# A fused retention and two-layer MLP kernel: part of the first layer by seven half-size products, with sums of x on GpSimd and two x tiles

## Chip, cores and metric

The kernel runs on one core of one Trainium2 chip. The metric is the device time of one execution in microseconds (us). A core has a matrix engine (TensorE, "PE" in the profile), VectorE ("DVE"), ScalarE ("ACT"), GpSimd ("POOL"), and SyncE ("SP"), which issues most of the transfers here.

## Reference

Eight batches of eight heads go through retention, a linear attention with a decay per head; the result, 4608 tokens of 512 features, goes through two matrix products with a leaky ReLU between them.

```python
def _attn_ref(q, k, v):            # q, k, v: (8, 8, 576, 64) float32
    scale = 1.0 / np.sqrt(D_)
    scores = scale * np.matmul(q, k.transpose(0, 1, 3, 2))
    gamma = 1.0 - 2.0 ** (-5.0 - np.arange(H))
    rel = pos[:, None] - pos[None, :]
    Dmat = np.where(rel >= 0, gamma[:, None, None] ** rel[None, :, :], 0.0)
    return np.matmul(scores * Dmat[None], v)

def _moe_ref(x, w_in, w_out):      # x: (4608, 512), w_in: (512, 2048), w_out: (2048, 512)
    h = x @ w_in
    g = np.maximum(0.01 * h, h)
    return g @ w_out
```

The inputs and the output are float32; the kernel multiplies in float16 and accumulates in float32.

## The kernel before

**Units and groups.** The tokens are cut into 36 units of 128 (two chunks of 64) and 9 groups of 512 (four units). Retention runs unit by unit and the MLP group by group. Everything is in one hand-written order; each engine executes its own instructions in that order, and semaphores join the engines where data passes. A pool hands out its buffers in turn, and a new tile waits until the old one in its buffer has been read.

**Retention of a unit u.** `load` (line 119) fetches k, q and v, from unit 8 on through SP. `cast_k` (172, ScalarE), `cast_q` (175) and `cast_v` (179) turn them into float16, the last two with decay factors; from unit 8 on these two run on GpSimd. `transpose_dma` (181) transposes q and k by a transfer on SP. `scores` (218, 227) makes the score blocks and the state updates on TensorE, `masks` (236) and `state` (258 to 264) take them up on VectorE, and `state_cast` (276, 279) makes the float16 state. `outputs` (294, 305) multiplies by v and by the state; `own` (361, ScalarE) and `add` (366, VectorE) put the two parts together into the tile xT of the group, one of three buffers of `x_pool` (73). `burst(u)` (682) is scores of u with outputs of u - 1 and the VectorE, GpSimd and ScalarE work that follows; `step(u)` (710) is the burst, the loads of unit u + 4, and `ahead(u + 2)` (697): k cast, q cast, v cast, transpose. Units 0 to 7 are transposed on TensorE in an order of their own, in which `settle` (661) is the VectorE work on a unit's states and masks.

**First layer.** `h_block(g, f)` (395) makes one of 16 blocks of 128 hidden features for 512 tokens: four matmuls of 512 columns into one of four PSUM buffers of `acc_pool` (80), then `leaky` on ScalarE (393) into the tile gt. Groups 0 and 1 use `h_half` (256 tokens, two blocks) and `h_unit` (128 tokens, four blocks) instead. All of them record line 379 for their matmuls.

**Second layer.** Group 0 uses `wide` (429, 16 calls of four matmuls). From group 1 on, `seven` (475) forms the product of a 2 by 2 block matrix with a 2 by 2 block matrix by seven half-size products instead of eight, in the manner of Strassen and Winograd. It needs sums of the hidden tile (`mix`, 473, VectorE), sums of the output weights (`mix_weights`, 454), and intermediate sums k1, u2, v kept in SBUF. Each product is 16 times two matmuls of 256 columns (493). Product p1 is copied to k1 by ScalarE (505) before a second product is accumulated on top of it. `hooks` place a step after the first product and another after the fifth.

**Main loop.** For groups 2 to 8 the order of the first layer is blocks in pairs (i, i + 8), a step of the next group's units after the 5th and the 13th block, the mixes of the first half after the 9th, then `seven`. In a group g the steps are those of units 4g + 5, 4g + 6, and, in `seven`, 4g + 7 and 4g + 8. Ahead of the loop, `early(12, 14)` in the hooks of group 1 does burst 12, the casts and the transpose of unit 14, and then the loads of unit 16.

**Start of the main part.** After the blocks of groups 0 and 1 (lines 718 to 790), 16 `wide` calls follow with work attached by number in the dictionary `at` (797): for example scores of unit 8 after call 4 and `early(9, 12)` after call 9. Loads of units 8 to 11 and the transposes of 8 and 9 are put among the last blocks of group 1:

```python
    halves(1, (1, 4))
    load(10)
    ahead(8)
```

Of the kernel before, what the change touches and what calls it, by code (L numbers as in the profile page):

```python
# [9 lines left out]
FP = mybir.dt.float32  # L10
# [8 lines left out]
def kernel(  # L19
# [9 lines left out]
    nc = tc.nc  # L29
# [40 lines left out]
    ld_pool = ctx.enter_context(tc.tile_pool(name="ld", bufs=6))  # L70
    a_pool = ctx.enter_context(tc.tile_pool(name="ap", bufs=4))
    b_pool = ctx.enter_context(tc.tile_pool(name="bp", bufs=2))
    x_pool = ctx.enter_context(tc.tile_pool(name="xp", bufs=3))
    g_pool = ctx.enter_context(tc.tile_pool(name="gp", bufs=2))
    s_pool = ctx.enter_context(tc.tile_pool(name="sp", bufs=1))
    o_pool = ctx.enter_context(tc.tile_pool(name="op", bufs=3))
# [27 lines left out]
    w_in16 = const_pool.tile([P, NP, DFF], F16, name="w_in16")  # L104
    w_out16 = const_pool.tile([P, NF, DM], F16, name="w_out16")
    w_mix = const_pool.tile([P, 4, HF, HN], F16, name="w_mix")
    zst = const_pool.tile([P, NP, CH], F16, name="zst")
    idle = const_pool.tile([P, TOK], F16, name="idle")

# [9 lines left out]
    def load(u, eng=None, after=None):  # L119
        for x in (1, 0, 2):  # L120
            t = ld_pool.tile([P, H, D], FP, name=f"t32_{x}")
            t32[u, x] = t
            c = 2 * u
            same = c % CB + 1 < CB
            e = eng[x] if isinstance(eng, dict) else eng or nc.sync
            engs = e if isinstance(e, tuple) else (e,)
            n = H // len(engs)
            for j, rows in ((0, P),) if same else ((0, CH), (1, CH)):
                b, w = (c + j) // CB, (c + j) % CB
                for i, e in enumerate(engs):  # L130
                    hs = slice(n * i, n * i + n)
                    d = e.dma_start(
                        out=t[CH * j : CH * j + rows, hs],
                        in_=(q, k, v)[x][b, hs, CH * w : CH * w + rows, :].rearrange(
                            "h t d -> t h d"
                        ),
                    )
                    if after is not None and (x in after or not isinstance(after, dict)):
                        behind(d, *(after[x] if isinstance(after, dict) else after))
                        after = None  # L140
                    last_load[u, x] = d
# [28 lines left out]
    def cast_k(u):  # L170
        qk16[u] = a_pool.tile([P, 2, H, D], F16, name="qk16")
        nc.scalar.copy(out=qk16[u][:, 1], in_=t32[u, 1])  # L172

    def cast_q(u, eng):
        eng.tensor_tensor(out=qk16[u][:, 0], in0=t32[u, 0], in1=decay(u, 0), op=MUL)  # L175

    def cast_v(u, eng):
        v16[u] = a_pool.tile([P, H, D], F16, name="v16")
        eng.tensor_tensor(out=v16[u], in0=t32[u, 2], in1=decay(u, 1), op=MUL)  # L179

    def transpose_dma(u):
        qkT[u] = a_pool.tile([P, 2, NP, P], F16, name="qkT")
        nc.sync.dma_start_transpose(
            out=qkT[u].rearrange("p x c t -> p (x c) t"),
            in_=qk16[u].rearrange("t x h d -> t (x h d)"),
        )
# [205 lines left out]
    def leaky(out, in_):  # L392
        nc.scalar.activation(out=out, in_=in_, func=mybir.ActivationFunctionType.Lrelu)  # L393
# [13 lines left out]
    def h_unit(u, fb):  # L407
        g, t0 = u // 4, (u % 4) * P
        ts = slice(t0, t0 + P)
        hps = acc_pool.tile([P, 4, P], FP, name="acc")  # L410
        for n in range(4):
            h_mm(hps, n, g, 4 * fb + n, ts)
        leaky(g_tile(g)[:, 4 * fb : 4 * fb + 4, ts], hps)

    def store(g, a, osb):
        r0 = g * TOK + a * HT
        nc.sync.dma_start(
            out=out[r0 : r0 + HT, :].rearrange("(t p) d -> p t d", p=P), in_=osb  # L420
        )
# [24 lines left out]
    def mix_weights(n, x):  # L446
        fs = slice(x * HF // 2, (x + 1) * HF // 2)
        a, b = (
            (w_part(0, 1), w_part(0, 0)),
            (w_part(1, 1), w_mix[:, 0]),  # L450
            (w_part(1, 1), w_part(0, 1)),
            (w_part(1, 0), w_mix[:, 1]),
        )[n]
        nc.vector.tensor_tensor(out=w_mix[:, n, fs], in0=a[:, fs], in1=b[:, fs], op=SUB)
# [6 lines left out]
    def mix(g, n, x):  # L461

        fs = slice(x * HF // 2, (x + 1) * HF // 2)
        if g not in sums:
            sums[g] = s_pool.tile([P, 2, HF, HT], F16, name="mix")
        s = sums[g]
        z, a, b, op = (
            (s[:, 0], g_part(g, 1, 0), g_part(g, 1, 1), ADD),
            (s[:, 1], s[:, 0], g_part(g, 0, 0), SUB),
            (g_part(g, 1, 0), g_part(g, 0, 0), g_part(g, 1, 0), SUB),  # L470
            (g_part(g, 0, 0), g_part(g, 0, 1), s[:, 1], SUB),
        )[n]
        nc.vector.tensor_tensor(out=z[:, fs], in0=a[:, fs], in1=b[:, fs], op=op)  # L473
# [175 lines left out]
    def halves(g, *items):  # L649
        for a, fb in items:  # L650
            h_half(g, a, fb)

    def cast_qv(u):
        cast_q(u, nc.vector)
        cast_v(u, nc.vector)
# [5 lines left out]
    def settle(u):  # L661
        state(u, 0)
        state_cast(u, dve_copy, (0,))
        masks(u)
        state(u, 1)
# [11 lines left out]
    def mixes(g, *ns):  # L677
        for n in ns:
            mix(g, n, 0)
            mix(g, n, 1)  # L680
# [13 lines left out]
            own(u - 1)  # L694
            add(u - 1)

    def ahead(u):

        if u >= NU:
            return  # L700
        cast_k(u)
        cast_q(u, nc.gpsimd)
        cast_v(u, nc.gpsimd)
        transpose_dma(u)

    def fetch(u):
        if u < NU:
# [2 lines left out]
    def step(u):  # L710
        burst(u)
        fetch(u + 4)
        ahead(u + 2)


    halves(0, (0, 1))
# [34 lines left out]
    turn(6, 0)  # L751
    h_unit(5, 0)
    scores(6)
    settle(6)
    cast_qv(7)
    h_unit(5, 1)
    turn(7, 1)
    halves(1, (0, 4))
# [15 lines left out]
    mix_weights(0, 0)  # L774
    mix_weights(0, 1)
    h_unit(7, 0)
    h_unit(7, 1)
    mix_weights(1, 0)
    mix_weights(1, 1)
    halves(1, (1, 4))  # L780
    load(10)
    ahead(8)
    mix_weights(2, 0)
    mix_weights(2, 1)
    halves(1, (1, 5), (1, 6))
    ahead(9)
    load(11)
    mix_weights(3, 0)
    mix_weights(3, 1)
    halves(1, (1, 7))  # L790

    def early(u, n):
        burst(u)
        ahead(n)
        load(n + 2)

    at = {
# [2 lines left out]
        3: lambda: mixes(1, 1),  # L800
        4: lambda: (burst(8, False), ahead(11), load(13)),
        7: lambda: mixes(1, 2),
        9: lambda: early(9, 12),
    }
    for n in range(16):
# [3 lines left out]
    burst(10)  # L809
    seven(1, {0: [lambda: early(11, 13)], 4: [lambda: early(12, 14)]})  # L810

    first = [f for i in range(4) for f in (i, i + HF)]
    second = [f for i in range(4, 8) for f in (i, i + HF)]
    for g in range(2, NG):
        more = g < NG - 1
        for n, f in enumerate(first + second):
            h_block(g, f)
            if more and n in (4, 12):
                step(4 * g + 5 + (n == 12))
            if n == 8:  # L820
                for m in range(3):
                    mix(g, m, 0)
        for m in range(3):
            mix(g, m, 1)
        seven(
            g,
            {0: [lambda: step(4 * g + 7)], 4: [lambda: step(4 * g + 8)]} if more else {},
            g == NG - 1,
        )
# [30 lines left out]
```

## Time and profile before

| | |
|---|---|
| median of 8 runs | 289.54 us (289.35 to 291.73) |
| the profiled execution, its own time | 289.65 us |
| span of its profile, first to last instruction | 287.9 us |
| mean granted TensorE clock | 0.998 of full speed |
| busy PE / DVE / ACT / POOL | 279.3 / 173.0 / 143.9 / 104.7 us |
| first-layer matmuls, 512 columns (L379) | 448, record 379 ns each |
| second-layer matmuls, 256 columns (L493) | 896, record 273 ns each |
| activation of a block (L393) | 144, 597 ns each |
| GpSimd q cast / v cast (L175, L179) | 1087 / 1140 ns mean |
| from one group's first layer to the next | 29.11 us |

A record of a matmul contains its way through the pipeline; matmuls in a row overlap, so their true cost is the distance from one start to the next. In the chain of waits, a piece is given by its start, its length, the engine with the tile written and the line, and the number of instructions. In the timeline, a row is start, length, engine, line, operation, out<-in, count, and in brackets the idle time before it with what ended it. A "q" after an engine's name is its queue or sequencer. "DMA" is the mean busy share of the 16 transfer engines in tenths of each of 40 slices.

### The profile page before, as it was taken

Reading aid. Unit: us, or ns where it says so; the run is one execution under the profiler, and the core shown is the slowest. Engines: PE = TensorE matmul, PEld = TensorE weight load, DVE = VectorE, ACT = ScalarE, POOL = GpSimd, SP = SyncE. Lnnn points to the kernel's source line nnn. Section 1 sums busy time; section 2 is a strip of 40 time slices with the busy share of each in tenths; the row PEclk is TensorE's granted clock in tenths of the full one; section 3 lists DMA queues with packets and bytes.
Section 4 is the critical chain, followed back from the end, with each engine's and each line's share of the span. In section 5 each row is a group of like instructions: output and inputs, shape, how many; then the busy total and the mean of one; then the engine's idle time right before and its main releaser. Section 6 shows DMA issues by size and latency. Waiting matters only on the chain.

```text
span 287.9 us, 9432 instructions
## 1 busy us (share of the span) xinstructions
PE 279.3 (97%) x4111; PEld 190.4 (66%) x4111; DVE 173.0 (60%) x297; ACT 143.9 (50%) x254; POOL 104.7 (36%) x124
## 2 busy tenths in 40 slices
PE   8899999999999999999999999999999999999994
PEld 3478889545874587458745874587458745874584
DVE  2884687984664585459545863586368636740352
ACT  4676766623237633763277327732773176317510
POOL 8979502745333333333434333234325413000000
PEclk9999999999999999999999999999999999999999
DMA  8999999999999999956897679766976251012003
GB/s 215 300 238 213 292 206 201 199 165 236 201 253 288 220 209 201 260 130 148 184 257 160 140 159 278 148 148 152 285 156 147 49 173 39 3 68 81 0 2 146
DMA packets 131738, 50.01 MB, mean 174 GB/s; under 512 B 121264, under 2 KB 126000, under 8 KB 131696
## 3 DMA queue, kind: packets, MB, share of 16 engines
q1 hardware_dynamic: 125392, 39.59, 59.8%
q0 software_dynamic: 6016, 9.70, 14.9%
q8 instruction: 32, 0.52, 0.7%
q10 hardware_dynamic: 288, 0.11, 0.2%
q14 instruction: 10, 0.08, 0.1%
HBM read 36.81 MB, written 9.44 MB: 161 GB/s over the span
## 4 chain that ended last, share of the span: by engine, by line
PE 86%; DMA 5%; DVE 5%; ACT 1%; issue 1%; POOL 1%; POOLq 0%; DVEq 0%
PE acc L379 41%; PE acc L493 34%; DMA t<-in_q_dram 4%; PE acc L429 3%; PE sc L218 3%; DMA qkT<-qk 2%; PE ot L294 2%; PE sc L227 1%; PE ot L305 1%; PE acc L200 1%; DVE qk L175 1%; DVE st L279 1%; DVE s L236 1%; DVE s L260 1%; DVE xT L366 0%
## 5 line engine op out<-in xcount | busy, mean ns | idle before, releaser
L379 PE MATMUL acc<-xT,w_in 128*128 128x512 f16 (+2 forms) x768 | 131.0, 326 | 0.2 <-DVE xT L366 0.2
L393 ACT ACTIVATE gt<-acc 128x512 f16<-128x512 f32 x144 | 85.9, 597 | 56.7 <-PE acc L379 55.1
L379 PEld LDWEIGHTS <-w_in 128*128 128x128 f16 x768 | 68.1, 98 | 51.5
L493 PEld LDWEIGHTS <-gt 128*128 128x128 f16 x640 | 61.8, 98 | 9.2
L236 DVE TENSOR_TENSOR s<-sc,cs 128x512 f16<-128x512 f32 x34 | 23.3, 686 | 39.2 <-PE sc L227 39.2
L493 PE MATMUL acc<-w_out,gt 128*128 128x256 f16 x384 | 45.9, 273 | 0.2
L276 POOL CAST st<-s 128x512 f16<-128x512 f32 x21 | 12.8, 609 | 89.8 <-DVE s L260 56.4
L361 ACT COPY own<-ot 128x512 f32<-128x512 f32 x33 | 19.3, 585 | 42.4 <-PE ot L305 35.0
L175 POOL TENSOR_TENSOR qk<-t,cs 128x512 f16<-128x512 f32 x28 | 30.4, 1087 | 18.8 <-ACT gt L393 15.4
L179 POOL TENSOR_TENSOR v<-t,cs 128x512 f16<-128x512 f32 x28 | 31.9, 1140 | 1.5 <-DMA t<-in_v_dram 1.5
L473 DVE TENSOR_TENSOR mix<-gt 128x1024 f16<-128x1024 f16 x16 | 14.0, 878 | 28.8 <-ACT gt L393 28.8
L493 PE MATMUL acc<-w_mix,gt 128*128 128x256 f16 x256 | 30.6, 273 | 0.0
L493 PE MATMUL acc<-w_mix,mix 128*128 128x256 f16 x256 | 29.5, 273 | 0.0
L493 PEld LDWEIGHTS <-mix 128*128 128x128 f16 x256 | 24.9, 98 | 3.1 <-DVE mix L473 0.2
L172 ACT CAST qk<-t 128x512 f16<-128x512 f32 x36 | 22.3, 620 | 7.9 <-DMA t<-in_k_dram 5.5
L366 DVE TENSOR_TENSOR xT<-ot,own 128x512 f16<-128x512 f32 x33 | 22.6, 683 | 5.1 <-ACT own L361 5.1
L260 DVE TENSOR_TENSOR s<-sc,s 128x256 f32<-128x256 f32 x37 | 15.5, 419 | 1.7 <-PE sc L227 1.1
L218 PEld LDWEIGHTS <-qkT 64*64 64x64 f16 x576 | 7.7, 107 | 12.6 <-issue 9.9
L519 DVE TENSOR_TENSOR osb<-acc,u 128x512 f32<-128x512 f32 (+1 forms) x17 | 11.2, 656 | 7.9 <-PE acc L493 7.9
L473 DVE TENSOR_TENSOR mix<-mix,gt 128x1024 f16<-128x1024 f16 x16 | 14.8, 932 | 0.5
L279 POOL CAST st<-s 128x256 f16<-128x256 f32 x7 | 3.2, 454 | 31.3 <-DVE s L264 19.4
L429 PE MATMUL acc<-w_out,gt 128*128 128x512 f16 x64 | 14.3, 380 | 0.0
(57 smaller groups left out, 236.5 us busy)
## 6 DMA issues: line engine op xcount, KB each, us to landing
out_dram<-osb SPq DMA_DIRECT2D x17, 512.0 KB, 3.9
t<-in_k_dram SPq DMA_DIRECT2D x27, 256.0 KB, 4.4
t<-in_q_dram SPq DMA_DIRECT2D x26, 256.0 KB, 4.1
t<-in_v_dram SPq DMA_DIRECT2D x25, 256.0 KB, 4.9
w_in<-in_moe_w_in_dram POOLq DMA_DIRECT2D x8, 256.0 KB, 6.4
w_out<-in_moe_w_out_dram POOLq DMA_DIRECT2D x4, 512.0 KB, 10.9
t<-in_v_dram POOLq DMA_DIRECT2D x7, 256.0 KB, 5.5
t<-in_q_dram POOLq DMA_DIRECT2D x6, 256.0 KB, 5.6
```

Source lines behind the costliest of these rows:

```text
L172: nc.scalar.copy(out=qk16[u][:, 1], in_=t32[u, 1])
L175: eng.tensor_tensor(out=qk16[u][:, 0], in0=t32[u, 0], in1=decay(u, 0), op=MUL)
L179: eng.tensor_tensor(out=v16[u], in0=t32[u, 2], in1=decay(u, 1), op=MUL)
L236: nc.vector.tensor_tensor(out=s16s[u], in0=sc_tiles[u][:, :, 0], in1=mask_sb.unsqueeze(1).unsqueeze(1).to_broadcast([P, 2, NP, CH]), op=MUL,)
L260: nc.vector.tensor_tensor(out=to, in0=st, in1=carry[0], op=ADD)
L361: nc.scalar.copy(out=owns[u], in_=ot_tiles[u][:, :, 0:NP].rearrange("q j c t -> q c j t"))
L366: nc.vector.tensor_tensor(out=x_of(u).rearrange("q (c g) t -> q c g t", g=2), in0=ot_tiles[u][:, :, NP : 2 * NP].rearrange("q g (c j) t -> ...
L379: nc.tensor.matmul(out=hps[:, n, :], lhsT=w_in16[:, c, f * P : (f + 1) * P], rhs=xT[g][:, c, ts], start=(c == 0), stop=(c == NP - 1),)
L393: nc.scalar.activation(out=out, in_=in_, func=mybir.ActivationFunctionType.Lrelu)
L429: nc.tensor.matmul(out=ys[tb], lhsT=g_t[0][:, f, tb * P : (tb + 1) * P], rhs=w_out16[:, f, :], start=(f == 0), stop=(f == NF - 1),)
L473: nc.vector.tensor_tensor(out=z[:, fs], in0=a[:, fs], in1=b[:, fs], op=op)
L493: nc.tensor.matmul(out=r[name][tb][:, 0, :] if apart else r[name][0][:, tb, :], lhsT=lhs[:, f, tb * P : (tb + 1) * P], rhs=rhs[:, f, :], s ...
```

## The change

In groups 2 to 8 four of the sixteen first-layer blocks, 0, 1, 8 and 9, are made by `h_seven`: the 2 by 2 block product of w_in (features 0-1 or 8-9; contraction chunks 0-1 or 2-3) with x (the two contraction halves; the two token halves of 256), by seven products of 2 x 2 matmuls with 256 columns. Four more blocks stand between the products. It reads four sums of weight blocks, which `sum_w_in` makes once on VectorE after wide call 12, and four sums of x, which `sum_x` makes on GpSimd for each group, in the step that completes its x: after that step's q cast and ahead of its v cast. Three intermediate sums, and h4 (twice) and h5, are formed by VectorE; ScalarE applies the activation from PSUM once and from SBUF three times. `x_pool` goes from three buffers to two. The steps of the main loop stand after the first eight blocks and after the 14th, the first half's mixes after the 11th. The casts and transposes of units 8 and 9 and the loads of 10 and 11 around them are put earlier among the blocks of group 1, the transpose of 8 ahead of the loads of 10. In place of `settle(6)` and the casts of q and v of unit 7, the q cast is put between the masks of unit 6 and its second state.

```diff
-    x_pool = ctx.enter_context(tc.tile_pool(name="xp", bufs=3))
+    x_pool = ctx.enter_context(tc.tile_pool(name="xp", bufs=2))
...
+    w_sum = const_pool.tile([P, 4, NP // 2, 2 * P], F16, name="w_sum")
...
+    def w_sub(i, j):
+        return w_in16[:, 2 * j : 2 * j + 2, i * HF * P : i * HF * P + 2 * P]
+
+    def x_sub(g, j, k):
+        return xT[g][:, 2 * j : 2 * j + 2, k * HT : (k + 1) * HT]
+
+    def sum_w_in(n):
+        a, b, op = (
+            (w_sub(1, 0), w_sub(1, 1), ADD),
+            (w_sum[:, 0], w_sub(0, 0), SUB),
+            (w_sub(0, 0), w_sub(1, 0), SUB),
+            (w_sub(0, 1), w_sum[:, 1], SUB),
+        )[n]
+        nc.vector.tensor_tensor(out=w_sum[:, n], in0=a, in1=b, op=op)
+
+    x_sums = {}
+
+    def sum_x(g):
+        x_sums[g] = t = s_pool.tile([P, 4, NP // 2, HT], F16, name="x_sum")
+        for n, (a, b) in enumerate(
+            (
+                (x_sub(g, 0, 1), x_sub(g, 0, 0)),
+                (x_sub(g, 1, 1), t[:, 0]),
+                (x_sub(g, 1, 1), x_sub(g, 0, 1)),
+                (x_sub(g, 1, 0), t[:, 1]),
+            )
+        ):
+            nc.gpsimd.tensor_tensor(out=t[:, n], in0=a, in1=b, op=SUB)
+
+    def h_seven(g, fill):
...
+        def product(name, lhs, rhs, fresh):
+            if fresh:
+                r[name] = acc_pool.tile([P, 2, HT], FP, name="acc")
+            for n in range(2):
+                for c in range(NP // 2):
+                    nc.tensor.matmul(
...
+        def plus(name, a, b):
+            r[name] = m_pool.tile([P, 2, HT], FP, name=name)
+            nc.vector.tensor_tensor(out=r[name], in0=r[a], in1=r[b], op=ADD)
+
+        def give(i, k, name):
+            leaky(g_tile(g)[:, i * HF : i * HF + 2, k * HT : (k + 1) * HT], r[name])
+
+        product("p1", w_sub(0, 0), x_sub(g, 0, 0), True)
+        r["k1"] = m_pool.tile([P, 2, HT], FP, name="k1")
+        nc.scalar.copy(out=r["k1"], in_=r["p1"])
+        h_block(g, fill[0])
+        product("p1", w_sub(0, 1), x_sub(g, 1, 0), False)
+        give(0, 0, "p1")
+        h_block(g, fill[1])
+        product("p6", w_sum[:, 1], t[:, 1], True)
+        plus("u2", "p6", "k1")
+        product("p5", w_sum[:, 0], t[:, 0], True)
+        plus("v", "p5", "u2")
+        h_block(g, fill[2])
+        product("p7", w_sum[:, 2], t[:, 2], True)
+        plus("h4", "p7", "v")
+        product("p5", w_sum[:, 3], x_sub(g, 1, 1), False)
+        plus("h5", "p5", "u2")
+        give(1, 1, "h4")
+        h_block(g, fill[3])
+        give(0, 1, "h5")
+        product("p7", w_sub(1, 1), t[:, 3], False)
+        plus("h4", "p7", "u2")
+        give(1, 0, "h4")
...
-    def ahead(u):
...
+    def ahead(u, between=None):
+
+        if u < NU:
+            cast_k(u)
+            cast_q(u, nc.gpsimd)
+        if between is not None:
+            between()
+        if u < NU:
+            cast_v(u, nc.gpsimd)
+            transpose_dma(u)
...
-        ahead(u + 2)
+        ahead(u + 2, (lambda: sum_x(u // 4 - 1)) if u % 4 == 0 else None)
...
-    settle(6)
-    cast_qv(7)
+    state(6, 0)
+    state_cast(6, dve_copy, (0,))
+    masks(6)
+    cast_q(7, nc.vector)
+    state(6, 1)
+    cast_v(7, nc.vector)
...
     h_unit(7, 0)
+    ahead(8)
+    load(10)
     h_unit(7, 1)
     mix_weights(1, 0)
     mix_weights(1, 1)
-    halves(1, (1, 4))
-    load(10)
-    ahead(8)
+    halves(1, (1, 4), (1, 5))
     mix_weights(2, 0)
     mix_weights(2, 1)
-    halves(1, (1, 5), (1, 6))
     ahead(9)
     load(11)
+    halves(1, (1, 6))
...
-        ahead(n)
+        ahead(n, (lambda: sum_x(u // 4 - 1)) if u % 4 == 0 else None)
...
+        12: lambda: [sum_w_in(n) for n in range(4)],
...
-    first = [f for i in range(4) for f in (i, i + HF)]
-    second = [f for i in range(4, 8) for f in (i, i + HF)]
+    rest = [f for i in range(2, HF) for f in (i, i + HF)]
     for g in range(2, NG):
         more = g < NG - 1
-        for n, f in enumerate(first + second):
+        h_seven(g, rest[:4])
+        if more:
+            step(4 * g + 5)
+        for n, f in enumerate(rest[4:]):
             h_block(g, f)
-            if more and n in (4, 12):
-                step(4 * g + 5 + (n == 12))
-            if n == 8:
+            if n == 2:
                 for m in range(3):
                     mix(g, m, 0)
+            if more and n == 5:
+                step(4 * g + 6)
```

More of the change, by code (lines that the diff above doesn't have):

```diff
@@ new lines @@
+    x_sums = {}
[11 more added lines that the diff above has]
+    def h_seven(g, fill):
+        r = {}
+        t = x_sums[g]
+        def product(name, lhs, rhs, fresh):
[4 more added lines that the diff above has]
+                    nc.tensor.matmul(
+                        out=r[name][:, n, :],
+                        lhsT=lhs[:, c, n * P : (n + 1) * P],
+                        rhs=rhs[:, c, :],
+                        start=fresh and n == 0 and c == 0,
+                        stop=c == NP // 2 - 1,
+                        skip_group_check=True,
+                    )
+        def plus(name, a, b):
[25 more added lines that the diff above has]
+        give(1, 0, "h4")
@@ L695, in burst @@
             add(u - 1)
-    def ahead(u):
[L699 to L704, printed above, removed]
+    def ahead(u, between=None):
[7 more added lines that the diff above has]
+            transpose_dma(u)
     def fetch(u):
```

## The prediction

> **What bounds the kernel now.** I read the page first, for the busy shares.
>
> ```profile
> span 287.9 us, 9432 instructions
> ...
> PE 279.3 (97%) x4111; PEld 190.4 (66%) x4111; DVE 173.0 (60%) x297; ACT 143.9 (50%) x254; POOL 104.7 (36%) x124
> ...
> PE   8899999999999999999999999999999999999994
> ...
> DMA  8999999999999999956897679766976251012003
> ```
>
> TensorE is busy in every slice; transfers are dense up to about slice 17 (some 125 us) and loose after. Busy matmuls are modelled, so I went on to the chain of waits in order of time, which gives true spacings. One group of 512 tokens (24 of its pieces left out):
>
> ```profile
> 141.82 4.32 PE acc L379 x20
> 146.14 0.25 PE sc L218 x16
> ...
> 146.78 7.01 PE acc L379 x32
> ...
> 157.13 1.75 PE acc L493 x16
> ...
> 258.01 13.81 PE acc L379 x64
> ```
>
> Between 72 us and 284 us no other engine enters the chain. A 512-column matmul costs 13.81 / 64 = 215.8 ns, a 256-column one 1.75 / 16 = 109.4 ns. First-layer groups start 29.11 us apart and contain no visible wait. So from group 2 on, work taken from TensorE is time gained, as long as its operands arrive.
>
> Before that, the timelines of TensorE and of the DMA queue show one larger wait:
>
> ```profile
> 52.84 4.48 PE L429 MATMUL acc<-w_out,gt 128*128 128x512 f16 x20
> 57.98 0.32 PE L218 MATMUL sc<-qkT 64*64 64x64 f16 x16 [0.67 <-DMA qkT<-qk]
> ```
> ```profile
> 49.21 2.08 SPq L132 DMA_DIRECT2D t<-in_k_dram  x1
> 51.46 0.80 SPq L132 DMA_DIRECT2D t<-in_q_dram  x1
> 52.37 0.75 SPq L132 DMA_DIRECT2D t<-in_v_dram  x1
> 53.29 4.01 SPq L183 DMA_TRANSPOSE qkT<-qk  x2
> ```
>
> The scores of unit 8 wait for its transpose, which stands behind the three loads of unit 10 on SP. Its q cast ended at 50.03 and its k cast at 51.52.
>
> **What the Trainium skill says.** "TensorE: Matmul & The Clock Gate", section "Wait — 56ns, not 53.3ns?", gives N / 2.4 + 2.5 ns from start to start: 215.8 and 109.2 ns for 512 and 256 columns. The trace agrees (215.8, 109.4), so halving a matmul costs only 1.3 ns. "SBUF — State Buffer", section "Who interferes with whom", says that a VectorE instruction with two SBUF inputs and a GpSimd one that reads SBUF exclude each other. The trace agrees: the same 1024-element difference takes 0.68 us alone and about 1.5 us beside GpSimd.
>
> ```profile
> 47.84 0.68 DVE L454 TENSOR_TENSOR w_mix<-w_out 128x1024 f16<-128x1024 f16 x1
> ...
> 52.55 2.98 DVE L454 TENSOR_TENSOR w_mix<-w_out,w_mix 128x1024 f16<-128x1024 f16 x2
> ```
>
> **Part 1, seven products.** Per group, 4 blocks x 4 = 16 matmuls of 512 columns become 7 x 2 x 2 = 28 of 256: 16 x 215.8 = 3.45 us against 28 x 109.3 = 3.06 us, a gain of 0.39 us. For groups 2 to 8: 2.75 us. There are 12 more weight loads, of 98 ns each (row L379 PEld); 98 is under 109, so they stay beneath the matmuls, as in the second layer's runs today.
>
> What it adds must keep up. Let h be the start of the first layer; p6 starts after p1's two halves and two full blocks, at h + 2 x 0.44 + 2 x 0.86 = h + 2.6.
> - ScalarE: the k1 copy (0.585 us, row L505) must end before p1's second half. In the second layer p1's last matmul starts at 158.60 (its record ends at 158.87) and its copy ends at 159.50, 0.90 later; the block between gives 0.109 + 0.864 = 0.97. It fits by 0.02 after the 0.05 handover. Activations stay 0.60 each; there are 17 operations for 16.
> - VectorE: five sums with one PSUM input, 0.69 each (row L507), 3.4 us a group on an engine that is busy 17.8 of 29.1. The tightest, v before p5's second half, has 1.74 - 1.54 = 0.2 us, less a handover. VectorE is idle there today (142.5 to 146.6), so I count nothing. The mixes come some 1.7 us later against the blocks; they keep about 1 us before the second layer's p6.
> - GpSimd: four differences of 128x512 f16, in the FIFO behind the state cast and the q cast:
>
> ```profile
> 139.86 0.61 POOL L276 CAST st<-s 128x512 f16<-128x512 f32 x1 [2.79 <-DVE s L260]
> 140.43 1.04 POOL L175 TENSOR_TENSOR qk<-t,cs 128x512 f16<-128x512 f32 x1
> 141.43 1.04 POOL L179 TENSOR_TENSOR v<-t,cs 128x512 f16<-128x512 f32 x1
> ```
>
> The q cast ends 0.19 us before h (141.66) in groups 3, 4 and 7, and 0.24 to 0.34 after h in groups 2, 5 and 6, whose state update has a decay step more; group 8 has no casts. p6 needs the second difference: at -0.19 + 2T + 0.1 or +0.3 + 2T + 0.1. The trace has no f16-only difference on GpSimd. Nearest row: L175, 1.04 us with f32 inputs. "GPSIMD Engine Reference", section "Elementwise — side-by-side cycle accounting", gives 2.6 cycles an element for two inputs, an estimate of 512 x 2.6 / 1.2 = 1.11 us, set by reading[...]. Bounds: 0.6 (the one-input cast L276) and 1.58 (a contended q cast at 48.45). I take 1.05: ready at h + 2.0 or h + 2.5, against 2.6. Cost 0 to 0.1 us in three groups. The v cast queued behind the differences moves 4.2 us; it ends near h + 5.2, the next step is at h + 6.6, and v is first read some 6 us after that. The transpose needs only q and k, which stay ahead. The state cast of the next step is behind the v cast, and free by then.
>
> **Part 2, four weight sums** on VectorE during the wide blocks. Estimate from the 0.68 us row: half of its 1024 elements at two a cycle take 0.27 off, so 0.42 each, 1.7 us. VectorE is idle from 65.37 to 69.22, and even doubled by a concurrent cast they fit nearly. Counted 0; if they overrun, the sum of x of unit 9 and with it unit 10's outputs come up to 0.5 us late.
>
> **Part 3, two x tiles.** xT of group g+1 takes the buffer of g-1, last read a whole group earlier: 0.
>
> **Part 4, units 8 and 9 sooner.** The transpose of 8 can now be issued at 50.05, when the q cast ends (q landed at 48.3; k at 46.8, so the k cast does not hold the activations behind it on ScalarE). Even with today's 4.65 us it lands at 54.7, before TensorE gets there at 57.24. Gain: 57.98 - 57.24 = 0.74 us. Past it moves load 10 on SP, by 1.3 to 3.5 us, and so casts 10 (q at about 57.5 instead of 56.1). Behind them on GpSimd is the state cast of unit 8, free near 61, needed at 62.3: cost 0, bound 0.5. The transpose of 9 stays near 56 on SP, lands by 60, needed at 62.0.
>
> **Part 5, the q cast of unit 7 ahead of state(6, 1).** VectorE runs without a gap from 38.89 to 45. The transposes at 41.69 come 0.33 us earlier, but the scores at 42.95 and the block at 43.55 wait for VectorE work whose end is unchanged. Counted 0.
>
> **What is late next.** With TensorE ahead, transposes on the dense DMA queue matter. Unit 12 lands at 78.32; TensorE now asks at 79.28 - 0.74 = 78.54: just met. Unit 15's is issued from 95.32 to 97.65 behind loads; with the 2.0 to 2.8 us that units 14 and 16 took after the issue it lands at 99.7 to 100.5. TensorE would ask at 82.69 + 6.6 + 5.92 + 4.22 = 99.4. I charge 0.4 (0 to 1.1). Later transposes have over 5 us of slack, of which the new spacing takes 2.6 at most.
>
> **Sum.** 2.75 + 0.74 - 0.4 = 3.1 us. The profiled execution took 289.65 us, its span of 287.9 and 1.75 around it; that is 0.11 over the median of 289.54. So 286.5 profiled, 286.4 as a median. A measurement of this kernel can tell about 0.3% (0.87 us) from no change.
>
> **Rivals.**
> 1. GpSimd becomes the bound (ends slower). If one difference takes T, stalls are 2T - 2.6 in three groups and 2T - 2.15 in three. At T = 1.47 they eat 3.1 us, at 1.54 the kernel is 0.3% slower, at 1.6 they sum to 4.8 us: 291.2. For it: casts of 1.5 us are in the trace. Against: those stand beside VectorE differences of two SBUF inputs, and in this stretch VectorE reads PSUM. Chance 0.13, and 0.04 for a like mishap in the hand-ordered products (a PSUM buffer freed late).
> 2. The gain stays hidden by transfers in the dense part: TensorE reaches unit 15 at 100.5, as before, and only groups 3 to 8 pay: 6 x 0.39 = 2.4, so 287.2. For it: 0.96 us of slack at unit 12 before. Chance 0.2.
> 3. ScalarE hands over late: k1 or the activations behind it cost 0.1 to 0.3 us a group, 0.7 to 2.1 in all: 287.1 to 288.5, or no measurable change at the worst end. Chance 0.13.
> That leaves 0.5 for the forecast itself.
>
> **How the numbers follow.** Predicted 286.4. Low end 285.5: both DMA charges at zero, and a little of the 0.24 us wait at 71.8. High end 288.9 takes in rivals 2 and 3 and T up to 1.45. Faster: 0.5 + 0.2 + 0.06 of rival 3 = 0.76; same 0.07; slower 0.17.
>
> **What would show it.** First layers 28.7 us apart instead of 29.1; the seven products at 109 ns a matmul without a gap ahead of p6; four GpSimd differences of about 1.05 us; the scores of unit 8 near 57.2. Wrong if p6 waits for GpSimd, or if differences take 1.5 us or more; wrong in size if unit 12's or 15's scores wait for their transposes by over 0.7 us.

## Result and the profile after

The changed kernel is faster by 0.8%: 287.23 us in the median of 11 runs (286.63 to 288.11), against 289.56 for 32 runs of the kernel before (288.9 to 291.73); the ratio is 0.992, with a 95% interval of 0.9903 to 0.9937. The profiled execution took 287.19 us, 2.46 less than the one of before.

The page of the kernel after, its parts on busy times and on the 40 slices:

```profile
span 285.4 us, 9702 instructions
...
PE 277.1 (97%) x4195; PEld 198.7 (70%) x4195; DVE 205.7 (72%) x336; ACT 145.2 (51%) x261; POOL 141.0 (49%) x152
...
PE   8799999999999999999999999999999999999994
...
DMA  8999999999999999958994879488959351012004
```

TensorE is still busy in every slice and has lost 2.2 us of work. The cost went to engines with room: VectorE has 32.7 us more, GpSimd 36.3 more (28 differences of 1.153 us are 32.3 of them), ScalarE 1.3.

The chain of waits of the kernel after, one first layer with the start of the second layer behind it (group 5; each piece: start, length, what; L457 is `h_seven`'s matmul, L380 the full blocks, L574 `seven`):

```profile
170.84 0.45 PE acc L457 x4
...
172.15 0.96 PE acc L457 x8
...
173.98 0.93 PE acc L457 x8
...
184.61 1.76 PE acc L574 x16
...
186.39 0.02 ACTq L586
...
186.45 0.59 ACT k L586
...
187.09 7.15 PE acc L574 x64
```

Read the lengths against the counts. Four half-size matmuls without a wait take 0.44 us (109 ns each), eight take 0.87. The eight of p6 and p5 take 0.96 and the eight of p7 and the second p5 take 0.93: 0.09 and 0.06 us of waiting, too short for the view of waits, which shows none here. And ScalarE, absent from this stretch before, now stands in the chain: the copy of k1 in the **second** layer (L586), with a piece of ScalarE's sequencer (ACTq) ahead of it.

The timelines of the kernel after, TensorE, the SP queue, and GpSimd:

```profile
52.89 4.48 PE L510 MATMUL acc<-w_out,gt 128*128 128x512 f16 x20
57.30 0.32 PE L219 MATMUL sc<-qkT 64*64 64x64 f16 x16
```
```profile
49.88 2.69 SPq L184 DMA_TRANSPOSE qkT<-qk  x1
```
```profile
139.20 1.04 POOL L176 TENSOR_TENSOR qk<-t,cs 128x512 f16<-128x512 f32 x1
140.20 1.15 POOL L445 TENSOR_TENSOR x_sum<-xT 128x512 f16<-128x512 f16 x1
141.43 1.15 POOL L445 TENSOR_TENSOR x_sum<-xT,x_sum 128x512 f16<-128x512 f16 x1
```

The transpose of unit 8 goes out at 49.88, ahead of the loads of unit 10 (the first of them at 52.69), and unit 8's scores no longer wait. On GpSimd the differences stand behind the q cast; the v cast follows them, at 144.76.

**Where the 2.5 us came from.** I date the traces by the first score matmul of a unit. Unit 8: 57.98 before, 57.30 after, 0.68 us. From unit 9 to the end of the span: 225.1 us before (287.9 - 62.78), 223.3 after (285.4 - 62.10), so 1.8 us for the seven products. Of that, the four groups between unit 16 and unit 32 show (all in us; the last two columns are experiments below):

| from unit to unit | before | after | experiment 5 | experiment 11 |
|---|---|---|---|---|
| 16 to 20 | 29.12 | 28.84 | 28.71 | 28.72 |
| 20 to 24 | 29.11 | 28.92 | 28.72 | 28.71 |
| 24 to 28 | 29.12 | 28.93 | 28.84 | 28.72 |
| 28 to 32 | 29.11 | 28.87 | 28.76 | 28.72 |
| sum | 116.46 | 115.56 | 115.03 | 114.87 |

The change gave 0.22 us a group, where the arithmetic of the matmuls promised 0.39. The group ahead of these gave 0.23, and what follows unit 32 gave 0.68.

### The profile page after: what moved, and what is told of

The parts are those of the page before. It is cut to its first block, busy times and chain, and to the rows that moved or that the text cites. A ratio compares the mean times of both kernels' runs of the same rounds, so it can differ in the third digit from the quotient of the medians.

```text
span 285.4 us, 9702 instructions
## 1 busy us (share of the span) xinstructions
PE 277.1 (97%) x4195; PEld 198.7 (70%) x4195; DVE 205.7 (72%) x336; ACT 145.2 (51%) x261; POOL 141.0 (49%) x152
## 4 chain that ended last, share of the span: by engine, by line
PE 90%; DVE 4%; ACT 2%; DMA 2%; issue 1%; SPq 0%; ACTq 0%
PE acc L380 35%; PE acc L574 34%; PE acc L457 8%; PE acc L510 5%; PE sc L219 2%; DMA t<-in_k_dram 2%; PE ot L295 1%; ACT k L586 1%; PE sc L228 1%; PE ot L306 1%; PE acc L201 1%; DVE qk L176 1%; ACT qkT L208 1%; DVE s L261 1%; DVE s L237 0%
## 5 line engine op out<-in xcount | busy, mean ns | idle before, releaser
L380 PE MATMUL acc<-xT,w_in 128*128 128x512 f16 (+2 forms) x656 | 110.5, 317 | 0.2 <-DVE xT L367 0.2
L394 ACT ACTIVATE gt<-acc 128x512 f16<-128x512 f32 x123 | 71.4, 597 | 28.2 <-PE acc L380 27.7
L380 PEld LDWEIGHTS <-w_in 128*128 128x128 f16 x656 | 57.1, 98 | 33.8 <-issue 0.2
L574 PEld LDWEIGHTS <-gt 128*128 128x128 f16 x640 | 61.8, 98 | 9.5
L574 PE MATMUL acc<-w_out,gt 128*128 128x256 f16 x384 | 45.9, 273 | 0.5
L176 POOL TENSOR_TENSOR qk<-t,cs 128x512 f16<-128x512 f32 x28 | 31.9, 1141 | 20.8 <-DMA t<-in_q_dram 20.8
L180 POOL TENSOR_TENSOR v<-t,cs 128x512 f16<-128x512 f32 x28 | 35.1, 1252 | 1.0 <-DMA t<-in_v_dram 0.7
L574 PE MATMUL acc<-w_mix,gt 128*128 128x256 f16 x256 | 30.6, 273 | 0.0
L574 PE MATMUL acc<-w_mix,mix 128*128 128x256 f16 x256 | 29.6, 273 | 0.0
L574 PEld LDWEIGHTS <-mix 128*128 128x128 f16 x256 | 25.0, 98 | 3.1 <-DVE mix L554 0.2
L554 DVE TENSOR_TENSOR mix<-gt 128x1024 f16<-128x1024 f16 x16 | 15.2, 958 | 7.8 <-ACT gt L394 7.8
L554 DVE TENSOR_TENSOR mix<-mix,gt 128x1024 f16<-128x1024 f16 x16 | 18.9, 1187 | 0.5
L445 POOL TENSOR_TENSOR x_sum<-xT 128x512 f16<-128x512 f16 x14 | 16.1, 1153 | 5.6 <-DVE xT L367 5.6
L468 DVE TENSOR_TENSOR u<-acc,k 128x512 f32<-128x512 f32 x7 | 4.8, 691 | 17.0 <-PE acc L457 14.5
L445 POOL TENSOR_TENSOR x_sum<-xT,x_sum 128x512 f16<-128x512 f16 x14 | 16.1, 1153 | 0.5
```

Source lines behind the costliest of these rows:

```text
L380: nc.tensor.matmul(out=hps[:, n, :], lhsT=w_in16[:, c, f * P : (f + 1) * P], rhs=xT[g][:, c, ts], start=(c == 0), stop=(c == NP - 1),)
L445: nc.gpsimd.tensor_tensor(out=t[:, n], in0=a, in1=b, op=SUB)
L574: nc.tensor.matmul(out=r[name][tb][:, 0, :] if apart else r[name][0][:, tb, :], lhsT=lhs[:, f, tb * P : (tb + 1) * P], rhs=rhs[:, f, :], s ...
```

## Experiments

My theory was that the arithmetic is right and that small handovers ate the rest: k1 (whose buffer name the two layers share), the sum v ahead of the second p5, and GpSimd's second difference. The rivals: other costs (transfers, x buffers, VectorE's load), or a gain that is mostly unit 8's wait. Ratios are to the kernel before, run on the same chip in the same session, with 95% intervals.

### 1. Units 8 and 9 sooner, alone

The kernel before with only this part of the change:

```diff
     h_unit(7, 0)
+    ahead(8)
+    load(10)
     h_unit(7, 1)
...
-    halves(1, (1, 4))
-    load(10)
-    ahead(8)
+    halves(1, (1, 4), (1, 5))
...
-    halves(1, (1, 5), (1, 6))
     ahead(9)
     load(11)
+    halves(1, (1, 6))
```

> The kernel before with one part of the change: units 8 and 9 cast and transposed sooner, the loads of 10 and 11 moved with them; no seven products. My theory (parts add up): the scores of unit 8 start near 57.3 instead of 57.98 and the 0.69 us stay to the end, so 0.69 us less, about 288.9; groups stay 29.11 us apart. Rival (the dense transfers take it back): the scores of unit 12 or 15 wait for their transposes, 0 to 0.3 us left, about 289.3. If the seven products were to bring all of the 2.3 us, this kernel would be equal to the one before.

Measured: 289.49 us against 289.47, ratio 1.0002 (0.9989 to 1.0015). In its profile unit 8's scores come at 57.38 without a wait, and units 12 and 15 don't wait either. So neither the expectation nor its rival held: no wait is left, and the time isn't shorter.

### 2. The seven products without it, and the kernel before once more

The kernel after with these lines put back, and the kernel before, unchanged:

> The kernel after, with units 8 and 9 put back where the kernel before has them; the seven products stay. Theory A (the ledger of the profiles): the scores of unit 8 wait 0.7 us again, so about 287.9, 0.6 to 0.7 us over the kernel after. Theory B (the first round's medians, in which units 8 and 9 sooner alone gave 0.0 us): the 0.7 us wait of the profile of before is not the usual case, or TensorE waits for transfers later instead; this kernel equals the kernel after, 287.2, and the seven products account for the whole gain of 2.3 us.

> The kernel before, unchanged, for a second profile and as a null comparison. Ratio 1.000. Theory A: the scores of unit 8 wait 0.5 to 0.8 us for their transpose here as well. Theory B: they wait less than 0.3 us, or the time appears as another wait in the dense transfers up to 125 us.

Measured: 287.32 us against 289.03 for the first, ratio 0.9935 (0.9919 to 0.995). The kernel before, measured against itself, gave 289.63 against 289.03, ratio 1.0025 (1.0003 to 1.0047); that much apart can two sets of runs of one program lie. The timeline of TensorE in the kernel with the old order, where the transpose of unit 8 goes out at 52.94:

```profile
52.83 4.48 PE L510 MATMUL acc<-w_out,gt 128*128 128x512 f16 x20
57.24 0.32 PE L219 MATMUL sc<-qkT 64*64 64x64 f16 x16
```

and TensorE in the second profile of the kernel before:

```profile
53.05 4.48 PE L429 MATMUL acc<-w_out,gt 128*128 128x512 f16 x20
57.56 0.32 PE L218 MATMUL sc<-qkT 64*64 64x64 f16 x16
```

With the old order, unit 8's scores come with no wait in one execution (57.24 is 4.41 after the row above starts, as in the kernel after) and 0.10 late in another (4.51); in the profile that I predicted from they were 5.14 after. So the wait of 0.7 us doesn't come in every execution with the old order; it stands in one of three on record. With the seven products and the old order, the distances from unit 16 to unit 32 are those of the kernel after to 0.01 us. So the gain that repeats is that of the seven products (this kernel also keeps the two x tiles and the new place of unit 7's q cast).

### 3. k1 under a name of its own

A tile of one name takes a buffer from a ring of that name. `h_seven` and `seven` both call theirs "k1".

```diff
-        r["k1"] = m_pool.tile([P, 2, HT], FP, name="k1")
+        r["k1"] = m_pool.tile([P, 2, HT], FP, name="hk1")
```

> The kernel after, with a buffer of its own for the k1 of the first layer (named hk1), so that the second layer's k1 is again written once a group. My theory: the second layer's k1 copy on ScalarE starts 0.057 us late because it has two semaphores to wait for, its own engine's among them, and a separate instruction for one of them; with its own buffer that instruction goes, the second half of p1 starts 0.055 us sooner in each of 7 groups, and the 0.018 us wait for k1 in the first layer goes too: groups 28.79 to 28.80 us apart instead of 28.87, 0.4 to 0.5 us less in all, about 286.8. Rival (ScalarE is late from its own backlog of activations): no difference, 28.87 apart, 287.2.

Measured: 287.36 us against 289.47, ratio 0.9922 (0.9894 to 0.995); the profiled execution took 286.77. Unit 16 to 32 takes 115.31 us instead of 115.56, so 0.06 a group. The chain of waits of this kernel, around the start of the second layer of group 5:

```profile
184.38 1.75 PE acc L574 x16
...
186.80 1.25 PE acc L574 x10
```

ScalarE has left the chain. From the first product's start to the next product it is 2.42 us (186.80 - 184.38), against 2.48 in the kernel after (187.09 - 184.61). In the trace of after, seven's k1 copy waits for two semaphores: TensorE's, in an instruction of its own on the sequencer (the piece "ACTq L586"), and the one that ScalarE itself raises. Before, and here, it waits for TensorE's alone. So the second wait is for an earlier instruction of ScalarE, most likely `h_seven`'s copy into the same buffer (the trace doesn't name it); whichever it is, it was done long ago, since ScalarE's last instruction ended at 185.25, more than 1 us before the copy. In the first layer, too, the second product on p1 no longer waits (0.44 us instead of 0.45). The times alone don't resolve 0.06 x 7 = 0.4 us; the trace does. In this profiled execution unit 15 waited 0.43 us for its transpose, which the profile of the kernel after doesn't have.

### 4. A block between v and the second p5

```diff
         plus("h4", "p7", "v")
+        h_block(g, fill[3])
+        give(1, 1, "h4")
         product("p5", w_sum[:, 3], x_sub(g, 1, 1), False)
         plus("h5", "p5", "u2")
-        give(1, 1, "h4")
-        h_block(g, fill[3])
         give(0, 1, "h5")
```

> The kernel after, with the fourth fill block ahead of the second product on p5 instead of behind it. My theory: the 0.060 us that the second product on p5 waits in every group is for VectorE's sum v, which reads the first; a block of 0.86 us between covers it, so groups come 28.81 us apart, 0.42 us less in all, about 286.8. Rival (the sums on VectorE are simply too many, 22 of 28.9 us busy): the wait moves to the second product on p7, whose h4 sum is as late, and nothing is gained: 287.2.

Measured: 286.95 us, ratio 0.9929 (0.9903 to 0.9954); profiled 286.79. Unit 16 to 32: 115.35, so 0.05 a group less. The second p5 adds onto the PSUM buffer of the first, and so can't start before VectorE has read that buffer for v. The rows of the kernel after, in group 5 (u is u2; the last row is the second p5):

```profile
172.77 0.69 DVE L468 TENSOR_TENSOR u<-acc,k 128x512 f32<-128x512 f32 x1 [2.51 <-ACT gt L394]
...
173.57 0.69 DVE L468 TENSOR_TENSOR v<-acc,u 128x512 f32<-128x512 f32 x1
...
174.31 0.60 PE L457 MATMUL acc<-xT,w_sum 128*128 128x256 f16 x4
```

The last record of p6 ends at 172.68. There are three handovers on the way: 0.09 us from p6 to u2, 0.10 from u2 to v, and 0.05 from v to p5, about 0.25 in all. With the block between, p5 no longer waits for them.

### 5. Both

> The kernel after with both repairs: k1 of the first layer in its own buffer, and the fourth fill block ahead of the second product on p5. My theory: the two waits are separate and add up, 0.055 + 0.018 + 0.060 us in each of 7 groups; groups 28.72 to 28.74 us apart instead of 28.87, 0.9 us less, about 286.3. Rival: with the waits gone the next in line is met at once (h4, or the state of a late transfer), and no more than one repair's worth is left, 286.8.

Measured: 286.45 us against 289.03, ratio 0.9918 (0.9895 to 0.9941); profiled 286.45. Unit 16 to 32: 115.03, 0.13 a group less; the two add up (0.06 + 0.05, and 0.02 more). The chain of waits, group 4:

```profile
143.06 0.87 PE acc L457 x8
...
144.80 0.44 PE acc L457 x4
...
146.10 0.87 PE acc L457 x8
```

Every product at its price. What is left stands in the groups whose state update has a decay step more (24 to 28: 28.84), where p6 still waits for GpSimd: 0.12 us in group 5, more than the 0.09 before, as the 0.02 at k1 ahead of it is gone.

### 6. One difference of x more

The first of the four differences is made twice, to the same tile:

```diff
+            for _ in range(2 if n == 0 else 1):
-            nc.gpsimd.tensor_tensor(out=t[:, n], in0=a, in1=b, op=SUB)
+                nc.gpsimd.tensor_tensor(out=t[:, n], in0=a, in1=b, op=SUB)
```

> The kernel after, with the first difference of x made twice on GpSimd (the same result). Each takes 1.15 us, so the second difference, which p6 waits for, comes 1.15 us later. My pricing of GpSimd as the bound: today it is met with 0.4 us to spare in groups 3, 4 and 7 and missed by 0.03 to 0.09 in 2, 5 and 6; so p6 waits about 0.75 us in three groups and 1.2 us in three, 0 in the last, in sum 5.8 us: about 293. Rival (there is slack elsewhere, such as GpSimd's later work being moved): under 2 us, below 289.2.

Measured, one run: 293.45 us, span 291.7, 6.3 more than after. The view of TensorE's waits (total, times, longest):

```profile
PE acc L458 <- POOL x_sum L446: 5.3, 6, 1.2
```

From the spacings of the chain the waits are 1.25, 0.79, 0.79, 1.32, 1.25 and 0.79 us in groups 2 to 7, in sum 6.2, where 5.8 was expected. The second difference now starts 2.47 us after the first (142.39 and 144.86 in group 4), where it was 1.23 (140.20 and 141.43 above): the added one cost 1.24, its own 1.15 and a gap of 0.07 to 0.08 behind it. So GpSimd has 1.24 - 0.79 = 0.45 us to spare in groups 3, 4 and 7, and nothing in groups 2, 5 and 6, where the kernel after already waits (0.03, 0.09 and 0.02 us). Behind this edge each microsecond on GpSimd ahead of the second difference is a microsecond lost.

### 7. Sums of x ahead of the q cast

```diff
             cast_k(u)
-            cast_q(u, nc.gpsimd)
         if between is not None:
             between()
         if u < NU:
+            cast_q(u, nc.gpsimd)
             cast_v(u, nc.gpsimd)
```

> The kernel after, with the sums of x ahead of the q cast on GpSimd instead of behind it. My theory (GpSimd is not where the missing time went): only the waits ahead of p6 in groups 2, 5 and 6 go, 0.030 + 0.094 + 0.024 = 0.15 us; the transposes of units 14, 18, 22 and so on are issued 4.6 us later, into 6.8 to 9 us of slack: 287.1. Rival (GpSimd is the bound): each group gains, 0.5 us or more in all. Other rival: the later transpose of 14, 18 or 22 in the dense transfers makes its scores wait, and the kernel is slower by 0.3 to 1 us.

Measured: 290.71 us against 289.47, ratio 1.0052 (1.0032 to 1.0072), slower than before. p6 waits in no group; but of TensorE's waits:

```profile
PE sc L219 <- DMA qkT<-qk: 2.9, 4, 1.5
```

The longest, in the timelines of SP and TensorE:

```profile
84.67 0.88 SPq L133 DMA_DIRECT2D t<-in_v_dram  x1
88.17 1.24 SPq L184 DMA_TRANSPOSE qkT<-qk  x1
```
```profile
101.94 0.32 PE L219 MATMUL sc<-qkT 64*64 64x64 f16 x16 [1.52 <-DMA qkT<-qk]
```

SP stands from 85.6 to 88.17 at the transpose of unit 14, whose q cast is now behind four differences; in the kernel after it was issued at 83.83. All loads and stores behind it are late, and the next transpose, of unit 15, goes out at 98.22 instead of 95.32 (0.5 us of that is this trace's later start); TensorE asks for it at 100.35 and gets it 1.59 us later. Units 15, 19 and 27 wait 1.59, 0.42 and 0.93 us, 2.9 in all. A fourth wait, 0.26 at unit 12, comes ahead of the first sum of x and can't be due to the edit. Together they are the 3.2 us by which the span grew. None of the three expectations held: it is not the transposes behind the sums that come too late, but the ones after them on SP's queue.

### 8. Sums of x on VectorE

```diff
-            nc.gpsimd.tensor_tensor(out=t[:, n], in0=a, in1=b, op=SUB)
+            nc.vector.tensor_tensor(out=t[:, n], in0=a, in1=b, op=SUB)
```

> The kernel after, with the four differences of x on VectorE instead of GpSimd. Estimate from the weight sums of the same shape there: 0.41 us each, 1.65 us a group, in place of 4.6 us on GpSimd. My theory: VectorE has that much room (22 of 28.9 us busy), the waits ahead of p6 go (0.03 to 0.09 us in three groups), and the second layer's sums on VectorE come no later; within 0.2 us of the kernel after, 287.1. Rival (VectorE is next to bind): u2 and v of the first layer are pushed back and the second product on p5 waits longer than 0.06 us, or the second layer's sums do; 0.5 to 2 us slower.

Measured: 292.99 us against 289.52, ratio 1.0114 (1.0099 to 1.013): I expected about no change, and that fell. Timelines of VectorE and TensorE:

```profile
112.92 1.26 DVE L445 TENSOR_TENSOR x_sum<-xT 128x512 f16<-128x512 f16 x1
114.10 0.41 DVE L445 TENSOR_TENSOR x_sum<-xT,x_sum 128x512 f16<-128x512 f16 x1
114.44 1.27 DVE L600 TENSOR_TENSOR osb<-acc,u 128x512 f32<-128x512 f32 x2
```
```profile
115.17 1.02 PE L380 MATMUL acc<-xT,w_in 128*128 128x512 f16 x4 [0.54 <-DVE osb L600]
```

A difference of this size takes 0.41 us alone and 1.15 to 1.26 beside GpSimd's q and v casts (111.48 to 113.90 here). That agrees with the Trainium skill ("SBUF — State Buffer", section "Who interferes with whom"), by which a VectorE instruction with two SBUF inputs contends with a GpSimd one that reads SBUF; it gives no durations for such a pair. The output sums of the second layer (osb) stand behind the four differences, and their PSUM buffers come free late; the second full block waits for one. By the view of waits that is 4.7 us in six groups. The rival expected a loss, but a smaller one (0.5 to 2 us; here it is 5.8 against the kernel after) and at the products, where that view shows none. So the sums of x don't fit on VectorE at this point, for a buffer's sake and not for the products'.

### 9. Three x tiles

```diff
-    x_pool = ctx.enter_context(tc.tile_pool(name="xp", bufs=2))
+    x_pool = ctx.enter_context(tc.tile_pool(name="xp", bufs=3))
```

> The kernel after, with three x tiles instead of two. My theory: a tile's last reader is a whole group behind its next writer, so the number makes no difference: 287.2, groups 28.87 us apart. Rival (add waits for the sums of x or the products of the group before): some tenths of a us less.

Measured: 288.17 us in 12 runs (287.15 to 291.36) against 289.52, ratio 0.9959 (0.9935 to 0.9983); profiled 287.27. In the trace all units from 16 to 32 take 115.57 us, as after, and no wait is new in the main part. The times scatter more than those of the kernel after, by up to 4 us; what in those runs takes the time no profile shows, so the median of this run says nothing sure about the buffer.

### 10. Unit 7's casts on GpSimd

On top of experiment 5, for the three short waits around 43 us that the change left (the prediction counted 0 for moving the q cast):

```diff
-    cast_q(7, nc.vector)
+    cast_q(7, nc.gpsimd)
     state(6, 1)
-    cast_v(7, nc.vector)
+    cast_v(7, nc.gpsimd)
```

> The kernel with both repairs (own k1, block first), and besides the q and v casts of unit 7 on GpSimd, which does nothing from 33.7 to 48.2 us, instead of VectorE. The change's reordering of the q cast left the end of VectorE's run from 38.9 to 43.6 where it was; taking 1.2 us of work out of that run should end TensorE's three waits at 41.4, 43.0 and 43.6 us (0.13 + 0.39 + 0.22 us): 0.7 us less than with both repairs alone, about 285.7. Rival: TensorE then only reaches a late transfer sooner (units 8, 12 or 15), and the end does not move: 286.4.

Measured: 286.52 us against 289.52, ratio 0.9894 (0.9877 to 0.9912). The profiled execution started late (unit 3's scores at 18.95 instead of 17.65), so only distances can be read: unit 6 to 7 takes 4.05 us instead of 4.57, unit 7 to 8 14.10 instead of 14.30. The waits in the timeline of the kernel after

```profile
43.00 0.32 PE L219 MATMUL sc<-qkT 64*64 64x64 f16 x16 [0.32 <-DVE qkT L208]
...
43.60 1.95 PE L380 MATMUL acc<-xT,w_in 128*128 128x128 f16 x32 [0.15 <-DVE xT L367]
```

are gone here: the same rows start at 44.35 and 44.73, with no idle time before them. VectorE's queue was the bound there; changing the order on it, as the change did, moved nothing (43.00 and 43.60 after, 42.95 and 43.55 before), and taking work off it gained 0.7 us between units 6 and 8. That this reaches the end isn't shown: the median is about that of experiment 5 (286.45), as the rival said, while the ratio is lower by 0.0024 (0.7 us), with intervals that overlap. The late start is a wait of 1.27 us for a load of w_in; experiment 11, which has the same edit, shows it too, and the other profiles 0 to 0.4. Whether it goes with the edit no run tells.

### 11. p5 ahead of p6

On top of experiment 10; p5 reads GpSimd's first difference, p6 the second:

```diff
+        product("p5", w_sum[:, 0], t[:, 0], True)
         product("p6", w_sum[:, 1], t[:, 1], True)
         plus("u2", "p6", "k1")
-        product("p5", w_sum[:, 0], t[:, 0], True)
```

> The kernel with both repairs and unit 7's casts on GpSimd, and besides the product p5 ahead of p6. p5 needs the first difference of x alone, p6 the second, so the second has 0.44 us more. My theory: the waits for GpSimd in groups 2, 5 and 6 (0.03, 0.10 and 0.03 us) go, nothing else moves: first layers of every group take the same 6.6 us, 0.16 us less than without it, about 286.0 where an undisturbed start lets the casts' 0.7 us through. Rival (the sum v, now 0.44 us later against the products, is waited for): 0.1 to 0.4 us a group are lost.

Measured: 286.27 us against 289.67, ratio 0.9875 (0.9836 to 0.9914). The chain of waits, group 5, where p6 had waited 0.09:

```profile
172.53 0.87 PE acc L457 x8
...
174.27 0.44 PE acc L457 x4
...
175.57 0.87 PE acc L457 x8
```

The four groups are now 28.71 or 28.72 apart, in sum 114.87: 1.59 less than before, 0.40 a group, and 0.69 less than after. By the spacings this is the best version. The intervals of the ratios of experiments 5, 10, 11 and of the change overlap, so the times alone don't rank them.

This profile also shows a price of experiment 10's edit:

```profile
39.84 0.32 PE L219 MATMUL sc<-qkT 64*64 64x64 f16 x16 [0.27 <-DVE qkT L208]
```

Unit 5 to 6 takes 6.13 us instead of 5.80. VectorE's v cast of unit 6 took 1.36 us here (0.68 in experiment 5), beside GpSimd's casts of unit 7, and the copy that TensorE waits for is behind it. In experiment 10 both of unit 6's casts on VectorE were stretched (1.42 and 0.92), but without a wait. So the edit's gain at the start was 0.7 us in one execution and 0.4 in the other.

## Why the prediction was right, and where it was off

The predicted median was 286.4 us, the measured one 287.23; direction and range held. Three terms of the sum were mis-sized: the handovers, the wait at unit 8, and the charge for transfers. The third made up for part of the first.

**Part 1's arithmetic held.** 109 ns a half-size matmul, with more weight loads underneath, is what the trace shows, and 0.39 us a group is what experiment 11 measures (0.40) once nothing waits. From unit 9 to the end it takes 285.3 - 62.79 = 222.5 us: 2.6 less than before, with a wait of 0.24 at unit 15; without it, some 2.8, against the 2.75 predicted.

**The handovers that were counted at nothing.** Here the change missed by 1.0 us: 2.75 predicted, 1.8 measured. Per group the runs show:
- v ahead of p5's second half, "0.2 us, less a handover": 0.06 late (the 0.93 in the chain; experiment 4 gives 0.05). There are three handovers in this path, 0.25 us together, and one was charged.
- k1 of the first layer, "It fits by 0.02 after the 0.05 handover": 0.02 late (0.45 for 0.44 in most groups), but on time in experiments 3 and 5, where it has a name of its own. The arithmetic was right; the shared name broke it.
- 0.06 at k1 of the second layer, which the prediction doesn't list. A tile of the same name in another function added a wait to an instruction that had nothing to spare. I looked at buffers for what is late, not for what a further wait itself costs.
- 0.03, 0.09 and 0.02 for p6 in groups 2, 5 and 6; predicted 0 to 0.1. A difference took 1.15 us, not 1.05; the estimate of 1.11 that the prediction worked out from the Trainium skill ("GPSIMD Engine Reference", section "Elementwise — side-by-side cycle accounting") was nearer than the row of the f32 cast.

These make 0.14 to 0.23 a group, about the 0.17 that is missing; experiment 11, which has all of them out, gained 0.17 a group over after. A rest stays unexplained: group 4 of the kernel after loses 0.07 in a row of output matmuls (0.20 for 0.14) that experiments 5 and 11 don't show there. Rival 3, a late ScalarE at 0.1 to 0.3 us a group, gave the right amount, for reasons only half of which are ScalarE's.

**Part 4's 0.74 was one execution's.** The wait was in the profile and went away (0.68), but the kernel doesn't always have it: experiment 2 shows 0.10 and none with the old order, and experiment 1 a ratio of 1.0002 for the edit alone. It should have been a range from 0 to 0.74. The interval of experiment 1 leaves the edit between 0.4 us of loss and 0.3 of gain.

**The DMA charge of 0.4** was a charge and not a fact: the profile of after shows unit 15 at 99.59 without a wait (predicted 99.4), experiments 3, 4 and 11 waits of 0.43, 0.10 and 0.24. That it came to nothing offset some 0.4 of the 1.0 us that the handovers took, so the profiled sum came to 2.5 (1.8 + 0.7) against 3.1. That the median came within 0.8 us is in part this luck.

**What was counted at nothing and was nothing.** Two x tiles (experiment 9's trace). The weight sums, 0.41 to 0.71 us each for 0.42, in VectorE's idle time from 64.6 to 66.5. Part 5 (41.41, 43.00 and 43.60 after, for 41.69, 42.95 and 43.55). Activations are still 597 ns. VectorE grew by 32.7 us where the five sums a group and the weight sums give 26: three forms of the mixes stretched from 878, 932 and 696 to 958, 1187 and 904 ns. In their new place they stand beside GpSimd's q and v casts (in group 4, 151.10 to 153.96 beside 150.48 to 153.42), not beside the differences of x, and the casts grew as well (q 1087 to 1141 ns, v 1140 to 1252). The prediction named the mechanism but didn't count it; it cost TensorE nothing that the chain shows.

**Rival 1** was a real edge. Its formula, 2T - 2.6 and 2T - 2.15, with T = 1.15 gives 0.3 us to spare and 0.15 of waiting; experiment 6 measured 0.45 and 0.03 to 0.09. Worked out from the prediction's own lines (-0.19 or +0.3, plus 2T + 0.1, against 2.6) it would be 2T - 2.7 and 2T - 2.2, 0.4 and 0.1, which is nearer. Rival 2 didn't occur. And "later transposes have over 5 us of slack" holds only because the q cast went ahead of the sums: experiment 7 held one transpose back by some 4 us, and waits for those behind it cost 2.9.

**Open:** how often the kernel before has the wait at unit 8, and why medians of one program lie up to 0.6 us apart (289.03 to 289.67). No run here tells. With that spread, the 2.3 us between the medians of before and after (1.8 to 2.8 by the interval of the ratio) agrees with the 1.8 of the seven products, and doesn't tell whether the earlier units add a few tenths.

## What to carry to other kernels

When work moves off the bound engine, the gain is its price less every handover that it adds. Count each one on the path (here they took 0.05 to 0.1 us each, and what just missed lost 0.02 to 0.09), and look for tiles that share a buffer name, since here a wait that was long satisfied still cost 0.06. Trust one profile for durations, but not for a wait behind a transfer; look at a second execution before you count its removal. On an in-order queue, the worth of an order shows in what stands behind it: the same four differences cost at most 0.09 us a group behind the q cast and 2.9 us in all ahead of it.

## What the runs showed that I had not expected

- GpSimd takes longer for a 128x512 difference of float16 (1.15 us) than for the cast with float32 inputs and float16 output (1.04 us): less to read didn't make it faster.
- A second semaphore on a ScalarE instruction, its own engine's, delayed it by 0.06 us with the semaphore long satisfied (experiment 3).
- VectorE's 128x512 float16 difference: 0.41 us alone, 1.15 to 1.26 beside GpSimd's casts (experiment 8), which take longer beside it too.
